# Sigmoid attention into a channel mix on one core: the first block of k in two pieces, narrower products of zeros, and the very last row block in two column halves

## The chip, the cores and the metric

The kernel runs on 1 core of one Trainium2 chip. The metric is the device time of one execution in microseconds (us). The profile is of one execution and counts from the first to the last instruction of the program (the span). Engines are named as the profile names them: PE is TensorE (PEld its weight loads), DVE VectorE, ACT ScalarE, POOL GpSimd, and SP, which here issues nearly all transfers.

## The reference

```python
scores = scale * np.matmul(q, k.transpose(0, 1, 3, 2)) - np.log(S)      # 8 batches, 12 heads, S 448, head 64
attn = 1.0 / (1.0 + np.exp(-scores))
x = np.matmul(attn, v)                                                   # then laid out as 8 x 448 x 768
x_prev = x shifted by one token, zeros first
xk = mu_k * x + (1.0 - mu_k) * x_prev
xr = mu_r * x + (1.0 - mu_r) * x_prev
k = np.maximum(xk @ w_k, 0.0)                                            # 768 -> 1024
v = k * k @ w_v                                                          # 1024 -> 768
r = 1.0 / (1.0 + np.exp(-(xr @ w_r)))                                    # 768 -> 768
return r * v
```

All arrays are float32 (the weights arrive as 64-bit words).

## The kernel before, in words

**Attention.** Two heads lie together in the 128 partitions of one tile, so there are 48 head pairs n; each has its tiles `kn`, `qn` and `vn` of 224 KB. For the first pair (`NATIVE = (0,)`) the scores are multiplied straight in float32; for all others k and q are split into a rounded high part and a low rest (`kh`, `kl`, `qh`, `ql`; type fp32r) and three products are added. `scores(n, c, u, at)` (L349) makes the scores of 128 keys (c = 0, 1, 2) against all 448 queries in the PSUM tile `sc[u]`; `sigmoid` (L373) is one ACT instruction over both heads' 896 columns; `score_tails` and `last_keys` do the last 64 keys of two pairs; `weigh` (L383), `weigh_tails` (L407) and `weigh_last` (L393) multiply with v into `av`; `gather` mixes neighbouring tokens on DVE and stores `xk` and `xr`. Beside it DVE converts the 64-bit weights.

**Channel mix.** Three stages, R (x w_r), K (x w_k), V (x w_v), each as a seven-product scheme for 2 x 2 blocks. A step is (stage, pair of token tiles, product p), with p in the order 0, 1, 5, 4, 6, 2, 3. A step has three row blocks i (four in stage K). `multiply` (L617) makes one row block: in stages R and K 3 x 3, in stage V 4 x 3 matmuls of 128 x 128 weights against T = 448 columns into one PSUM bank (`xb[i]` or `yb[i]`). `yb` gathers the products 0 + 5 + 6 + 3: p = 0 lands in `xb` and ACT copies it to `yb`, the others add to `yb` in place. `evacuate` and `finish` take a finished bank out: in stage V, DVE multiplies it with the stored sigmoid `r` (L648) and SP sends the tile to `out`. The last step is stage V, p = 3; its last row block is `yb[2]`. `yb[3]` is a bank that stage V leaves unused.

**What sets the order.** Nearly every instruction is an `Op` with an engine, an assumed cost, a due time and the tiles that it reads and writes. `Plan.order` plays these through on a list scheduler and the program is emitted in that order; each engine then executes its own list strictly in order and waits on semaphores. So a change of one cost or one added transfer can shift the order of later instructions on any engine. Outside of the plan stand, at the very start, a memset of `warm` (128 x 2, L152), a memset of `mk[1]` (128 x 448, L426), and two matmuls of zeros on 384 columns of `mk[1]` (L428) that keep PE busy until data are there. Then `load(0, ...)` fetches k of the first pair through SP's queue and q through ACT's.

Of the kernel before, what the change touches and what calls it, by code (L numbers as in the profile page):

```python
# [23 lines left out]
class Plan:  # L24
# [9 lines left out]
    def op(self, engine, cost, prio, run, reads, writes, dma=None, gate=False, opens=None):  # L34
        i = len(self.ops)
        deps = set()
        for r in reads:
            if r in self.writer:
                deps.add(self.writer[r])
        for w in writes:  # L40
            if w in self.writer:
                deps.add(self.writer[w])
            deps.update(self.readers.get(w, ()))
        for r in reads:
            self.readers.setdefault(r, []).append(i)
        for w in writes:
            self.writer[w] = i
            self.readers[w] = []
        deps.discard(i)
        self.ops.append(Op(engine, cost, prio, run, deps, dma, gate, opens))  # L50
# [58 lines left out]
def attention_then_channel_mix(  # L109
# [15 lines left out]
    nc = tc.nc  # L125
    P = 128
# [6 lines left out]
    T = S  # L133
# [5 lines left out]
    NJH, NFH = NJ // 2, NF // 2  # L139
# [11 lines left out]
    warm = const.tile([P, 2], F32, name="warm")  # L151
# [13 lines left out]
    WK_PACE, WV_PACE = 1.5, 1.5  # L165
    CAST_DVE = lambda n, a: n % 2 == 1
    NATIVE = (0,)

    def ring(pool, name, bufs, shape, dtype):
        return [pool.tile(shape, dtype, name=f"{name}{i}") for i in range(bufs)]  # L170
# [18 lines left out]
    kn = ring(apool, "kn", RAW, [P, S], F32)  # L189
    vn = ring(apool, "vn", 5, [P, NV, D], F32)  # L190
    gap(apool, "gap1", 64)
    qn = ring(apool, "qn", RAW, [P, S], F32)
# [10 lines left out]
    mk = ring(apool, "mk", 2, [P, S], F32)  # L203
    mr = ring(apool, "mr", 2, [P, S], F32)
    gap(apool, "gap4", 128)
    sc = ring(pscore, "sc", 3, [P, 2, 512], F32)
# [4 lines left out]
    op = plan.op  # L211
    SP, PE, ACT, DVE, POOL = "SP", "PE", "ACT", "DVE", "POOL"
    SWITCH = 92

    def mm(n, cols=S):
        return n * max(cols / 2.4 + 2.5, 200)

    def act(n, sbuf=False, ptr=False):
        return 100 + 0.834 * n + 42 * sbuf + 93 * ptr
# [10 lines left out]
    def dma(dst, src, prio, reads, writes, e="SP"):  # L230
        ns = dst.shape[0] * math.prod(dst.shape[1:]) * 4 / 300
        q_ = nc.scalar if e == ACT else nc.sync
        op(e, 500, prio, lambda: q_.dma_start(dst, src), reads, writes, dma=ns)
# [79 lines left out]
    def load_v(n, at):  # L313
        dma(vn[n % 5], v[n], at, [], [("vn", n % 5)])

    def load(n, at, e="SP", with_v=True):
        dma(kn[n % RAW], k[n], at, [], [("kn", n % RAW)])
        dma(qn[n % RAW], q[n], at, [], [("qn", n % RAW)], e)
        if with_v:
            load_v(n, at)  # L320

    def prepare(n, at):
        if n in NATIVE:
            return
# [8 lines left out]
    half = [slice(h * D, (h + 1) * D) for h in range(2)]  # L333
# [4 lines left out]
    def scores(n, c, u, at):  # L338
        i, m = n % LEAD, n % RAW
        if n in NATIVE:  # L340
            pairs, cost, reads = ((kn[m], qn[m]),), 752, [("kn", m), ("qn", m)]
        else:
            pairs, cost = ((kh[i], qh[i]), (kl[i], qh[i]), (kh[i], ql[i])), 602
            reads = [(a, i) for a in ("kh", "kl", "qh", "ql")]

        def go():
            for e, (kk, qq) in enumerate(pairs):
                for h in range(2):
                    nc.tensor.matmul(sc[u][:, h, :S], kk[half[h], c * P:(c + 1) * P], qq[half[h], :], start=e == 0, stop=e == len(pairs) - 1)  # L349

        pe(cost + 2 * SWITCH * (n % 2 == c == 0), go, reads, [("sc", u, 0), ("sc", u, 1)], at)
# [70 lines left out]
            dma(to[j][:, cols], m, at, [M], [("x", stage, j, b)])  # L422


    zeros = mk[1]
    nc.vector.memset(zeros, 0.0)  # L426
    for _ in range(2):
        nc.tensor.matmul(sc[0][:, 0, :3 * P], zeros[:, :P], zeros[:, :3 * P], start=True, stop=True)  # L428
    load(0, -9, ACT, False)
    op(ACT, 1500, -8.5, lambda: nc.scalar.activation(warm[:, 1:], warm[:, :1], AF.Sigmoid), [], [])  # L430
    load(1, -8, with_v=False)
    load_v(0, -7.8)
# [72 lines left out]
    e = N % RAW  # L505
# [17 lines left out]
    xb, yb = ([[None, (a, i)] for i in range(4)] for a in ("xb", "yb"))  # L523
# [14 lines left out]
    def tokens(tile_):  # L538
        return slice(tile_ * T, (tile_ + 1) * T)
# [63 lines left out]
    def slot_keys(g):  # L603
        return [("slot", g, h) + x for h in range(3) for x in ((), ("lo",))]

    def multiply(stage, s, p, i, at):
        g = POS[p]
        b = (yb if p in (5, 6, 3) else xb)[i]
        rs_ = used[stage, s, p]
        w = CW[stage]  # L610

        def go():
            n = len(rs_)
            for t, (rh, rl, _, _) in enumerate(rs_):
                hi, lo = (slots[g][:, a * n * w + t * w + i * P:a * n * w + t * w + (i + 1) * P] for a in range(2))
                for e, (l, r) in enumerate(((hi, rh), (hi, rl), (lo, rh))):
                    nc.tensor.matmul(b[0], l, r, start=p in (0, 4) and (t, e) == (0, 0), stop=(t, e) == (n - 1, 2), skip_group_check=True)  # L617

        op(PE, mm(3 * len(rs_), T), at, go, [k for r in rs_ for k in r[2:]] + slot_keys(g), [b[1]])


    def finish(stage, s, half, par, i, src, R, c, at):
        in_sbuf = c is not None
        if not in_sbuf:
            u = ncc[0] % len(cc)
            ncc[0] += 1
            c, C = cc[u]
        else:
            C = R[0]
        rows = KT[R_] if stage != K_ else NFH  # L630
        m, tile_ = half * rows + i, PAIRS[s][par]
        cols = tokens(tile_)
        if stage == R_:
            op(ACT, act(T, in_sbuf), at, lambda: nc.scalar.activation(c, src(), AF.Sigmoid), R, [C])
            dma(r_d[m][:, cols], c, at, [C], [("r", m, tile_)])
        elif stage == K_:
            if in_sbuf and half == 0:
                op(DVE, dve(T), at, lambda: nc.vector.scalar_tensor_tensor(c, src(), 0.0, src(), ALU.max, ALU.mult), R, [C])
            else:
                op(ACT, act(T, in_sbuf), at, lambda: nc.scalar.activation(c, src(), AF.Relu), R, [C])  # L640
                op(ACT, act(T, True), at, lambda: nc.scalar.activation(c, c, AF.Square), [C], [C])
            dma(k2_d[m][:, cols], c, at, [C], [("x", V_, m, tile_)])
        else:
            v_ = nrt[0] % len(rt_)
            nrt[0] += 1
            r, G = rt_[v_]
            dma(r, r_d[m][:, cols], at - 1.5, [("r", m, tile_)], [G])
            op(DVE, dve(T), at, lambda: nc.vector.tensor_mul(c, src(), r), R + [G], [C])  # L648
            dma(out[m * P:(m + 1) * P, cols], c, at, [C], [])

    def evacuate(stage, s, p, i, at):
        (_, X), (_, Y), (u, U), (f, F) = (z[i] for z in (xb, yb, u2, p4))
        x, y = (lambda: xb[i][0]), (lambda: yb[i][0])
        if p == 0:
            op(ACT, act(T), at, lambda: nc.scalar.copy(y(), x()), [X], [Y])  # L655
        elif p == 1:
            finish(stage, s, 0, 0, i, x, [X], None, at)
        elif p == 5:
            op(ACT, act(T), at, lambda: nc.scalar.copy(u, y()), [Y], [U])  # L659
        elif p == 4:  # L660
            op(ACT, act(T), at, lambda: nc.scalar.copy(f, x()), [X], [F])
        elif p == 6:
            op(DVE, dve(T), at, lambda: nc.vector.tensor_add(f, y(), f), [Y, F], [F])
            finish(stage, s, 1, 1, i, lambda: f, [F], f, at)
        elif p == 2:
            op(DVE, dve(T), at, lambda: nc.vector.tensor_add(u, x(), u), [X, U], [U])
            finish(stage, s, 0, 1, i, lambda: u, [U], u, at)
        elif p == 3:
            finish(stage, s, 1, 0, i, y, [Y], None, at)

    PREP, EVAC = -1.2, 0.3
    steps = [(stage, s, p) for stage in (R_, K_, V_) for s in range(len(PAIRS)) for p in ORDER]
    first = {stage: next(i for i, x in enumerate(steps) if x[0] == stage) for stage in (R_, K_, V_)}
    last = {(stage, p): max(i for i, x in enumerate(steps) if x[0] == stage and x[2] == p) for stage in (R_, K_, V_) for p in range(7)}
    for stage, w, out7, pace in ((K_, w_k, wk_o, WK_PACE), (V_, w_v, wv_o, WV_PACE)):
        at = OFF + first[stage - 1]
# [3 lines left out]
    for step, (stage, s, p) in enumerate(steps):  # L680
        at = OFF + step
        if (stage, s, p) not in used:
            right(stage, s, p, at + PREP)
        rows = NFH if stage == K_ else NJH
        if step == 3:
            reopen(psa, "pb4", "left", xb[3:] + yb[3:], AV)
        for i in range(rows):
            multiply(stage, s, p, i, at + i / rows)
            evacuate(stage, s, p, i, at + i / rows + EVAC)
        if stage < V_ and last[stage, p] == step:  # L690
            load_weight(stage + 1, p, OFF + max(step + 1.5, first[stage + 1] - 8 + POS[p]))
    ctx.enter_context(tc.manual_schedule())
# [41 lines left out]
```

## Time and profile before

| | |
|---|---|
| median of 3 runs | 807.07 us (806.75, 807.07, 808.11) |
| the profiled execution's own time | 807.04 us |
| its span | 805.0 us |
| PE busy | 800.0 us (99% of the span), 5146 matmuls |
| DVE busy | 620.2 us (77%) |
| ACT busy | 496.8 us (62%) |
| mean granted TensorE clock | 0.999 |
| DMA | 179.76 MB, mean 223 GB/s |

The profile's timeline merges instructions of one kind that follow each other: "x42" after a row means that 42 of them lie between the start and the start plus the duration given. A bracket at a row's end gives the time that the engine was idle before it, and what ended that. "DMA to landing" counts from the issue to the last landing. Bare names such as `pf` or `kn` are tiles without their buffer number.

### The profile page before, as it was taken

How to read it: one execution, taken by the hardware profiler on the slowest of the kernel's cores; microseconds unless marked ns; L12 is line 12 of the kernel's file. 1: busy time of each engine (PE TensorE's matmuls, PEld its weight loads, DVE VectorE, ACT ScalarE, POOL GpSimd, SP SyncE). 2: the span in 40 equal slices, each digit the busy share in tenths (PEclk: the TensorE clock that was granted, in tenths of full speed). 3: DMA queues.
4: the chain of work that ended last, by engine and by line, in shares of the span. 5: the costliest groups of instructions: out<-in, count | busy, mean ns of one | idle time of the engine just before them, and what ended most of it. 6: DMA issues, size and time to landing. Idle time of an engine off the chain costs nothing.

```text
span 805.0 us, 14663 instructions
## 1 busy us (share of the span) xinstructions
PE 800.0 (99%) x5146; PEld 652.7 (81%) x5146; DVE 620.2 (77%) x1161; ACT 496.8 (62%) x857; POOL 8.8 (1%) x29
## 2 busy tenths in 40 slices
PE   9999999999999999999999999999999999999998
PEld 4555555555557999999999999999999999999997
DVE  5888988899898998899988738356597594875944
ACT  6887878877786655556785655657774434344341
POOL 0000000000000000000000000000000000000000
PEclk9999999999999999999999999999999999999999
DMA  8878788798997776768787733434585546655415
GB/s 287 303 235 290 244 257 290 242 315 285 312 320 251 284 234 265 252 216 304 251 292 239 238 118 131 144 109 152 188 265 180 162 158 215 196 193 149 150 46 170
DMA packets 104761, 179.76 MB, mean 223 GB/s; under 512 B 11888, under 2 KB 93296, under 8 KB 104688
## 3 DMA queue, kind: packets, MB, share of 16 engines
q1 hardware_dynamic: 104544, 178.61, 67.3%
q8 instruction: 40, 0.66, 0.3%
q14 instruction: 33, 0.27, 0.1%
q10 hardware_dynamic: 144, 0.23, 0.1%
HBM read 109.06 MB, written 69.73 MB: 222 GB/s over the span
## 4 chain that ended last, share of the span: by engine, by line
PE 99%; DVE 0%; issue 0%
PE pb L617 69%; PE av L383 13%; PE sc L349 10%; PE av L407 2%; PE sc L358 2%; PE av L349 2%; PE av L393 1%; PE sc L428 0%; DVE pt L648 0%; DVE mk L426 0%; DVE warm L152 0%
## 5 line engine op out<-in xcount | busy, mean ns | idle before, releaser
L617 PE MATMUL pb<-rr,slot 128*128 128x448 f32 x2076 | 436.9, 362 | 0.0
L617 PEld LDWEIGHTS pb<-rr,slot 128*128 128x128 f32 x2076 | 389.1, 187 | 26.7 <-issue 0.7
L617 PE MATMUL pb<-qh,slot 128*128 128x448 f32 x464 | 152.6, 363 | 0.0
L383 PE MATMUL av<-pf,vn 64*64 64x448 f32 x1104 | 118.3, 544 | 0.0
L373 ACT ACTIVATE pf<-sc 128x896 f32<-128x896 f32 x120 | 103.9, 961 | 3.2 <-PE sc L349 3.2
L617 PEld LDWEIGHTS pb<-qh,slot 128*128 128x128 f32 x464 | 87.1, 188 | 5.7
L383 PEld LDWEIGHTS av<-pf,vn 64*64 64x64 f32 x1104 | 38.7, 132 | 60.6 <-issue 36.4
L617 PE MATMUL pb<-ql,slot 128*128 128x448 f32 x232 | 83.5, 360 | 0.0
L556 ACT CAST rr<-ys 128x448 fp32r<-128x448 f32 x66 | 36.4, 568 | 47.0 <-PE pb L617 45.1
L557 DVE TENSOR_TENSOR rr<-ys,rr 128x448 fp32r<-128x448 f32 x66 | 39.0, 619 | 12.0 <-ACT rr L556 11.9
L617 PEld LDWEIGHTS pb<-ql,slot 128*128 128x128 f32 x232 | 43.4, 187 | 3.0
L349 PE MATMUL sc<-qh,kh 64*128 64x448 f32 x236 | 45.4, 381 | 0.0
L557 DVE TENSOR_TENSOR rr<-pf,rr 128x448 fp32r<-128x448 f32 x38 | 23.2, 622 | 28.3 <-ACT rr L556 28.3
L417 ACT COPY xx<-av 128x448 f32<-128x448 f32 x48 | 23.3, 539 | 32.3 <-PE av L383 25.3
L349 PE MATMUL sc<-ql,kh 64*128 64x448 f32 x236 | 43.0, 361 | 0.0
L349 PE MATMUL sc<-qh,kl 64*128 64x448 f32 x236 | 42.7, 359 | 0.0
L418 DVE TENSOR_TENSOR dx<-xx 128x448 f32<-128x448 f32 x48 | 29.9, 623 | 14.8 <-ACT xx L417 14.8
L659 ACT COPY pf<-pb 128x448 f32<-128x448 f32 x40 | 21.3, 532 | 32.3 <-PE pb L617 30.2
L655 ACT COPY pb<-pb 128x448 f32<-128x448 f32 x40 | 20.7, 518 | 33.0 <-PE pb L617 33.0
L556 ACT CAST rr<-vn 128x448 fp32r<-128x448 f32 x50 | 27.9, 564 | 18.9 <-PE pb L617 17.6
L349 PEld LDWEIGHTS sc<-qh,kh 64*128 64x128 f32 x236 | 22.1, 184 | 18.2 <-issue 15.5
L557 DVE TENSOR_TENSOR rr<-vn,rr 128x448 fp32r<-128x448 f32 x50 | 29.6, 621 | 6.8 <-ACT rr L556 6.7
(113 smaller groups left out, 1034.1 us busy)
## 6 DMA issues: line engine op xcount, KB each, us to landing
kn<-in_k SPq DMA_DIRECT2D x48, 224.0 KB, 3.9
vn<-in_v SPq DMA_DIRECT2D x48, 224.0 KB, 4.6
xr_d<-mr SPq DMA_DIRECT2D x48, 224.0 KB, 4.7
xk_d<-mk SPq DMA_DIRECT2D x48, 224.0 KB, 4.6
pf<-r_d SPq DMA_DIRECT2D x48, 224.0 KB, 3.3
qn<-in_q SPq DMA_DIRECT2D x47, 224.0 KB, 4.3
k_d<-pf SPq DMA_DIRECT2D x34, 224.0 KB, 2.0
r_d<-pf SPq DMA_DIRECT2D x28, 224.0 KB, 2.4
```

What stands on the lines that cost most here:

```text
L349: nc.tensor.matmul(sc[u][:, h, :S], kk[half[h], c * P:(c + 1) * P], qq[half[h], :], start=e == 0, stop=e == len(pairs) - 1)
L358: nc.tensor.matmul(sc[u][half[m % 2], h, :S], kn[m % RAW][half[h], KW:], qn[m % RAW][half[h], :], start=True, stop=True)
L373: op(ACT, 815, at, lambda: nc.scalar.activation(f, sc[u][:, :, :S], AF.Sigmoid, bias=NEG_LOG_S, scale=SCALE), R, K, opens=opens)
L383: nc.tensor.matmul(av[m % 2][half[h], :S], vn[m % 5][half[r], h * NC + c, :], pf[(m * NC + c) % PFB][half[r], h, :], start=(turn, c) == (0 ...
L407: nc.tensor.matmul(av[r][half[h], :S], vn[(n + h) % 5][half[r], 2 * NC, :], pt[n // 2 % PTB][half[r], h, :], start=False, stop=stop, skip_ ...
L417: op(ACT, act(S), at - 1, lambda: nc.scalar.copy(x[:, 1:], av[n % 2][:, :S]), [AV[n % 2]], [X])
L418: op(DVE, dve(S), at, lambda: nc.vector.tensor_sub(d, x[:, 1:], x[:, :S]), [X], [G])
L556: op(ACT, act(T, True), at, lambda: nc.scalar.copy(hi, y), [Y], [H], gate=True)
L557: op(DVE, dve(T), at, lambda: nc.vector.tensor_sub(lo, y, hi), [Y, H], [L])
L617: nc.tensor.matmul(b[0], l, r, start=p in (0, 4) and (t, e) == (0, 0), stop=(t, e) == (n - 1, 2), skip_group_check=True)
L655: op(ACT, act(T), at, lambda: nc.scalar.copy(y(), x()), [X], [Y])
L659: op(ACT, act(T), at, lambda: nc.scalar.copy(u, y()), [Y], [U])
```

## The change

Three edits:

- **Start.** The matmuls of zeros read one element of `warm` in broadcast, as weights and as moving data, on 320 columns instead of 384. The memset of `mk[1]` is gone. The first k is fetched in two pieces, 128 columns (64 KB) and 320 columns (160 KB); the scores of c = 0 need the first piece alone, those of c = 1 and 2 also the second (key `("kn", 0, 1)`).
- **End.** The last row block of the last step is multiplied in two halves of 224 columns, the first in `yb[2]`, the second in `yb[3]`, each with its own DVE multiplication and its own transfer to `out`. For this ACT copies the right half of the partial sum from `yb[2]` to `yb[3]` two steps before.
- The stored sigmoid of that row block is fetched in two halves as well.

```diff
+    ZEROS = 320
...
+        if n == 0 and c > 0:
+            reads.append(("kn", 0, 1))
...
-    zeros = mk[1]
-    nc.vector.memset(zeros, 0.0)
     for _ in range(2):
-        nc.tensor.matmul(sc[0][:, 0, :3 * P], zeros[:, :P], zeros[:, :3 * P], start=True, stop=True)
-    load(0, -9, ACT, False)
+        nc.tensor.matmul(sc[0][:, 0, :ZEROS], warm[:, :1].to_broadcast([P, P]), warm[:, :1].to_broadcast([P, ZEROS]), start=True, stop=True)
+    dma(qn[0], q[0], -9, [], [("qn", 0)], ACT)
+    dma(kn[0][:, :P], k[0][:, :P], -9, [], [("kn", 0)])
+    dma(kn[0][:, P:], k[0][:, P:], -9, [], [("kn", 0, 1)])
...
+    def multiply(stage, s, p, i, at, cols=slice(0, T), b=None):
         g = POS[p]
-        b = (yb if p in (5, 6, 3) else xb)[i]
+        b = b or (yb if p in (5, 6, 3) else xb)[i]
+        c = cols.stop - cols.start
...
+                    nc.tensor.matmul(b[0][:, :c], l, r[:, cols], start=p in (0, 4) and (t, e) == (0, 0), stop=(t, e) == (n - 1, 2), skip_group_check=True)
...
+    def finish(stage, s, half, par, i, src, R, c, at, part=slice(0, T)):
...
+        cols = slice(tile_ * T + part.start, tile_ * T + part.stop)
+        c = c[:, :part.stop - part.start]
...
+            r = r[:, :part.stop - part.start]
...
         for i in range(rows):
+            if step == len(steps) - 1 and i == rows - 1:
+                for b, cols in ((yb[i], slice(0, T // 2)), (yb[NFH - 1], slice(T // 2, T))):
+                    multiply(stage, s, p, i, at + i / rows, cols, b)
+                    finish(stage, s, 1, 0, i, lambda b=b: b[0][:, :T // 2], [b[1]], None, at + i / rows + EVAC, cols)
+                continue
             multiply(stage, s, p, i, at + i / rows)
             evacuate(stage, s, p, i, at + i / rows + EVAC)
+            if step == len(steps) - 3 and i == rows - 1:
+                a, b = yb[i], yb[NFH - 1]
+                op(ACT, act(T // 2), at + i / rows + EVAC, lambda a=a, b=b: nc.scalar.copy(b[0][:, :T // 2], a[0][:, T // 2:]), [a[1]], [b[1]])
```

The order moves on ACT, DVE and SP in many places, because the plan's times shift by one transfer; on PE it stands as it was but for the first and the last rows. Three places matter for the prediction.

ACT at the start, before (`pf0` to `pf2` are the sigmoids of the first pair, `pt0` those of the last keys of two pairs, `pf3` to `pf5` those of the second pair; `kh0<-kn2` rounds k of the third):

```order
L373 ACTIVATE pf2_169<-av0_189 128x896
L373 ACTIVATE pt0_176<-sc0_186 128x896
L373 ACTIVATE pf3_170<-sc1_187 128x896
L373 ACTIVATE pf4_171<-sc2_188 128x896
L373 ACTIVATE pf5_172<-sc0_186 128x896
L225 CAST kh0_162<-kn2_145 128x384
L225 CAST qh0_157<-qn2_155 128x448
```

The same place after:

```order
L377 ACTIVATE pf2_169<-av0_189 128x896
L377 ACTIVATE pt0_176<-sc0_186 128x896
L226 CAST kh0_162<-kn2_145 128x384
L377 ACTIVATE pf3_170<-sc1_187 128x896
L377 ACTIVATE pf4_171<-sc2_188 128x896
L377 ACTIVATE pf5_172<-sc0_186 128x896
L226 CAST qh0_157<-qn2_155 128x448
```

The cast of the third pair's k has moved ahead of the three sigmoids of the second pair.

SP's queue at the start, before:

```order
L233 DMA kn0_143<-in_k 128x448
L233 DMA kn1_144<-in_k 128x448
L233 DMA qn1_154<-in_q 128x448
L233 DMA vn0_147<-in_v 128x448
L233 DMA vn1_148<-in_v 128x448
```

The whole first k is one issue, with k and q of the second pair behind it. The same queue after:

```order
L234 DMA kn0_143<-in_k 128x128
L234 DMA kn0_143<-in_k 128x320
L234 DMA kn1_144<-in_k 128x448
L234 DMA qn1_154<-in_q 128x448
L234 DMA vn0_147<-in_v 128x448
L234 DMA vn1_148<-in_v 128x448
```

One more issue stands ahead of everything else in that queue.

PE at its end, before (`pb5` is `yb[2]`; `rr`, `qh` and `ql` hold the moving data):

```order
L617 MATMUL pb5_2818<-rr4_128,slot6_122 128x448 x3
L617 MATMUL pb5_2818<-rr5_129,slot6_122 128x448 x3
L617 MATMUL pb5_2818<-qh0_157,slot6_122 128x448
L617 MATMUL pb5_2818<-ql0_159,slot6_122 128x448
L617 MATMUL pb5_2818<-qh0_157,slot6_122 128x448
L617 MATMUL pb5_2818<-qh1_158,slot6_122 128x448
L617 MATMUL pb5_2818<-ql1_160,slot6_122 128x448
L617 MATMUL pb5_2818<-qh1_158,slot6_122 128x448
```

These are twelve matmuls, each with a load of its weights. After, the same twelve stand twice, at 224 columns (`pb41` is `yb[3]`; six rows of the sixteen, where the first half ends and the second begins):

```order
L623 MATMUL pb5_2814<-qh1_158,slot6_122 128x224
L623 MATMUL pb5_2814<-ql1_160,slot6_122 128x224
L623 MATMUL pb5_2814<-qh1_158,slot6_122 128x224
L623 MATMUL pb41_2852<-rr4_128,slot6_122 128x224 x3
L623 MATMUL pb41_2852<-rr5_129,slot6_122 128x224 x3
L623 MATMUL pb41_2852<-qh0_157,slot6_122 128x224
```

The weights of the row block are loaded twice, 24 loads instead of 12.

More of the change, by code (lines that the diff above doesn't have):

```diff
@@ L604, in slot_keys @@
         return [("slot", g, h) + x for h in range(3) for x in ((), ("lo",))]
-    def multiply(stage, s, p, i, at):
+    def multiply(stage, s, p, i, at, cols=slice(0, T), b=None):
         g = POS[p]
-        b = (yb if p in (5, 6, 3) else xb)[i]
+        b = b or (yb if p in (5, 6, 3) else xb)[i]
+        c = cols.stop - cols.start
         rs_ = used[stage, s, p]
@@ L616, in go @@
                 for e, (l, r) in enumerate(((hi, rh), (hi, rl), (lo, rh))):
-                    nc.tensor.matmul(b[0], l, r, start=p in (0, 4) and (t, e) == (0, 0), stop=(t, e) == (n - 1, 2), skip_group_check=True)
-        op(PE, mm(3 * len(rs_), T), at, go, [k for r in rs_ for k in r[2:]] + slot_keys(g), [b[1]])
-    def finish(stage, s, half, par, i, src, R, c, at):
+                    nc.tensor.matmul(b[0][:, :c], l, r[:, cols], start=p in (0, 4) and (t, e) == (0, 0), stop=(t, e) == (n - 1, 2), skip_group_check=True)
+        op(PE, mm(3 * len(rs_), c), at, go, [k for r in rs_ for k in r[2:]] + slot_keys(g), [b[1]])
+    def finish(stage, s, half, par, i, src, R, c, at, part=slice(0, T)):
         in_sbuf = c is not None
@@ L631, in finish @@
         m, tile_ = half * rows + i, PAIRS[s][par]
-        cols = tokens(tile_)
+        cols = slice(tile_ * T + part.start, tile_ * T + part.stop)
+        c = c[:, :part.stop - part.start]
         if stage == R_:
```

## The prediction, written before the changed kernel was run

> **What bounds the kernel now.** I read the page first, for the busy shares and the chain that ended last.
>
> ```profile
> span 805.0 us, 14663 instructions
> PE 800.0 (99%) x5146; PEld 652.7 (81%) x5146; DVE 620.2 (77%) x1161; ACT 496.8 (62%) x857; POOL 8.8 (1%) x29
> PE 99%; DVE 0%; issue 0%
> ```
>
> The chain is PE from end to end. A busy PE need not be a PE at its pace, so I read next the view of waits for PE alone, which has one row, and the timeline of the channel mix, which has long merged pieces.
>
> ```profile
> PE sc L428 <- DVE mk L426: 1.4, 1, 1.4
> ```
> ```profile
> 786.69 8.39 PEld L617 LDWEIGHTS pb<-rr,slot 128*128 128x128 f32 x42
> 786.89 8.56 PE L617 MATMUL pb<-rr,slot 128*128 128x448 f32 x42
> ```
>
> PE waits for another engine only before its first product of zeros (a load's idle time, as in rows below, lies under the matmul ahead of it). In the channel mix 42 loads take 8.39 us, so one matmul of 448 columns passes every (8.39 − 0.19) / 41 = 0.20 us without a gap. Between the first score and the last matmul PE therefore works at its pace; time can be won or lost at the two ends, or by a new stall.
>
> **The start.** The timeline's first microseconds:
>
> ```profile
> 0.73 0.41 ACTq L233 DMA_DIRECT2D qn<-in_q  x1
> 0.74 0.86 SPq L233 DMA_DIRECT2D kn<-in_k  x2
> 0.81 0.06 DVE L152 MEMSET warm<- 128x2 f32 x1 [0.81 <-PEq L704]
> 0.93 0.43 DVE L426 MEMSET mk<- 128x448 f32 x1
> ...
> 1.42 2.93 PE L428 MATMUL sc<-mk 128*128 128x384 f32 x4 [1.42 <-DVE mk L426]
> ...
> 2.22 0.34 PEld L428 LDWEIGHTS sc<-mk 128*128 128x128 f32 x1 [0.30 <-issue]
> ...
> 2.86 0.34 PEld L428 LDWEIGHTS sc<-mk 128*128 128x128 f32 x1 [0.30 <-issue]
> ...
> 4.27 0.51 PEld L349 LDWEIGHTS sc<-qn,kn 64*128 64x128 f32 x4 [1.08 <-DMA qn<-in_q]
> ...
> 4.73 0.36 DVE L225 CAST kh<-kn 128x384 fp32r<-128x384 f32 x1 [3.37 <-DMA kn<-in_k]
> ...
> 5.12 0.56 DVE L330 TENSOR_TENSOR kl<-kn,kh 128x384 fp32r<-128x384 f32 x1
> ...
> 6.02 0.63 DVE L330 TENSOR_TENSOR ql<-qn,qh 128x448 fp32r<-128x448 f32 x1
> 6.05 0.19 PEld L349 LDWEIGHTS av<-qn,kn 64*128 64x128 f32 x2 [0.18 <-issue]
> 6.43 0.19 PEld L349 LDWEIGHTS av<-qn,kn 64*128 64x128 f32 x2 [0.18 <-issue]
> ```
>
> and PE's loads alone from 4.6 on, which keeps the first scores' pairs apart:
>
> ```profile
> 4.44 0.34 PEld L349 LDWEIGHTS sc<-qn,kn 64*128 64x128 f32 x2
> 5.18 0.30 PEld L349 LDWEIGHTS sc<-qn,kn 64*128 64x128 f32 x2 [0.40 <-issue]
> 5.67 0.19 PEld L349 LDWEIGHTS sc<-qn,kn 64*128 64x128 f32 x2 [0.18 <-issue]
> ```
>
> The first score starts at 4.27, when q has landed; k is not named as the last. The products of zeros fill the time until then: their passes are 0.64 us apart (2.22 to 2.86), the last ends near 2.22 + 3 x 0.64 = 4.14. The loads of the first scores are 0.38 us apart at the end (6.05 to 6.43), but here 0.74 (4.44 to 5.18) and then 0.49 (to 5.67): PE runs at half its clock until about 5.41 (the 0.49 are 0.23 at the slow rate and 0.26 at the fast one), 3.99 us after its first work.
>
> *Zeros.* The memset of 0.43 us goes and PE may start after the small one, at 0.81 + 0.06 + 0.05 = 0.92 instead of 1.42. A pass has 320 columns instead of 384, 0.53 us; the zeros end at 0.92 + 0.69 + 3 x 0.53 = 3.2. Broadcast operands appear in no row; their pass costs the 0.53 or, bounded by the old one, 0.64, which only fills idle time. Neither memset nor zeros are on the path, which waits for q.
>
> *k in pieces.* q waits beside k for the same DMA engines. Between 4.34 and 5.40 they move 365 GB/s:
>
> ```profile
> 4.34:5.40 1.06, 1.06 (x5) 0.66 (x6) 0.64 (x2) 0.00 (x0) 0.00 (x0) 1.00 1.04 365
> ```
>
> If the second piece (160 KB) came wholly behind q, q would land 0.44 us earlier; if it shares with q as all of k does now, 0. The second piece is issued 0.4 us later than the first, so part of it follows q: I take the middle, 0.2, the first score at 4.07. PE is at half clock there, so 0.2 us of head start is 0.1 us of work: **−0.1** (0 to −0.2). SP's extra issue (0.43) delays those of kn1 and the rest; the cover is the full DMA queue: kn1, issued at 1.17, lets DVE go only at 4.73. Without that cover, DVE's first casts come 0.4 later, and PE needs them only at 8.18.
>
> *The cast that moved on ACT.* This step is not in the diff but in the order. The place in the timeline before:
>
> ```profile
> 8.18 0.19 PEld L349 LDWEIGHTS sc<-qh,kh 64*128 64x128 f32 x2 [0.70 <-ACT pf L373]
> 8.29 0.19 PEld L349 LDWEIGHTS sc<-qh,kl 64*128 64x128 f32 x2
> ...
> 9.16 2.53 ACT L373 ACTIVATE pf<-sc 128x896 f32<-128x896 f32 x3
> ...
> 10.20 0.21 PEld L383 LDWEIGHTS av<-pf,vn 64*64 64x64 f32 x8 [0.31 <-issue]
> ...
> 11.55 0.53 ACT L225 CAST kh<-kn 128x384 fp32r<-128x384 f32 x1
> ...
> 11.95 0.60 ACT L225 CAST qh<-qn 128x448 fp32r<-128x448 f32 x1
> ```
>
> ACT runs without a gap from pt0 to pf5. The products with v at 10.20 need pf0 and pf3; pf3 is the first of the three from 9.16, spaced (2.53 − 0.92) / 2 = 0.80, done at 10.08. That leaves 0.1 us. The cast, 0.40 us to the next start (11.55 to 11.95), now goes ahead of pf3: pf3 is done at 10.48 and the products wait about 0.3 us. pf4 and pf5 come 0.4 later too but are wanted 0.8 apart behind that stall, so they add nothing. **+0.3** (0, if PE has slack there that I do not see, to +0.4). Nothing gives it back, since PE has no other wait to shorten.
>
> *The other moved instructions* of DVE, ACT and SP: nothing. Their cover is that PE waits for none of them anywhere; where it is gone, one stall is one DVE operation, 0.6.
>
> **The end.** The last 7 us:
>
> ```profile
> 798.89 1.36 PE L617 MATMUL pb<-rr,slot 128*128 128x448 f32 x6
> ...
> 801.09 0.37 PE L617 MATMUL pb<-qh,slot 128*128 128x448 f32 x1
> 801.49 0.62 DVE L648 TENSOR_TENSOR pt<-pb,pf 128x448 f32<-128x448 f32 x1 [1.78 <-PE pb L617]
> ```
> ```profile
> 802.90:803.00 0.10, 0.00 (x0) 0.00 (x0) 0.00 (x0) 0.00 (x0) 0.00 (x0) 1.00 0.27 108
> 803.00:803.75 0.75, 0.00 (x0) 0.00 (x0) 0.00 (x0) 0.00 (x0) 0.00 (x0) 1.00 0.76 292
> 803.75:804.10 0.35, 0.00 (x0) 0.00 (x0) 0.00 (x0) 0.00 (x0) 0.00 (x0) 1.00 0.00 0
> ```
>
> The twelve matmuls of the last row block start at 798.89, the last at 801.09; DVE starts 0.40 behind that, ends at 802.11, and the transfer moves its bytes from 803.00 to 803.75.
>
> *Matmuls.* Twice twelve of 224 columns. Their streaming takes half of 0.19, but each needs a load of 128 x 128 weights. No row has so narrow a matmul. From below: after an idle stretch the second load starts 0.11 us after the first (8.18 to 8.29), so loads cannot follow faster. From above: 0.20, if the pace belongs to the pair and not to the columns. I take 0.12: nearest is the load, 0.11, and the 0.20 holds 0.013 over the 0.1875 that a float32 pass of 448 columns takes (0.375 for two passes, 6.05 to 6.43). The last one starts at 798.89 + 23 x 0.12 = 801.65, and DVE 0.40 − 0.09 = 0.31 behind, at 801.96: +0.47.
>
> *DVE.* 384 columns take 0.56 and 448 take 0.63, 0.07 for 64, so 224 columns save 0.23. *Transfer.* Half the bytes in as many rows: between 0 and half of 0.75 are saved, I take 0.25. The sum of the end is 0.47 − 0.23 − 0.25 = **0.0**; with the bounds from 0.19 − 0.23 − 0.37 = −0.4 (0.11 a matmul) to 2.31 − 0.23 − 0.25 = +1.8 (0.20).
>
> *Beside it.* The first half's multiplication and transfer lie under the second half's matmuls. The added copy on ACT follows its last cast:
>
> ```profile
> 787.09 0.57 ACT L556 CAST qh<-pf 128x448 fp32r<-128x448 f32 x1
> ```
>
> It has 11 us until 798.89. The second half of `r` follows the multiplication of row block 0 (its buffer) and is wanted at 801.96. Both cost 0; each would cost its lateness.
>
> **Sum.** 807.04 (the profiled execution, 805.0 of span and 2.04 around it, 0.03 under the median of 807.07) − 0.1 + 0.3 + 0.0 = **807.2 us**.
>
> **Rivals.**
>
> *The clock comes later (slower).* Before, PE was busy from 1.42 to 5.41 with at most 0.3 us of gap when it got its full clock. After, it idles from 3.2 to 4.07, 0.85 us. If that gap starts the count afresh, full clock comes 3.99 us after 4.07, at 8.06 instead of 5.41: 2.65 us at half rate, +1.3, 808.5. It decides if the gap is long enough to spoil the count, which no row shows. The Trainium skill, "TensorE: Matmul & The Clock Gate", section "Part 1: The HAM clock gate (the "warmup" mystery)", says that the full clock comes after a busy window of about 3.4 us and that these windows run freely, not from the kernel's start; an estimate by it is up to a whole window at half rate, +1.7, against nothing by my sum, and a spread of that size between runs. The trace agrees as far as 3.99 us lies near it.
>
> *Narrow matmuls keep 0.20 us.* Then the end costs +1.8 and the time is 809.0. For it: 0.20 is the only pace of fp32r in the channel mix. Against: the 0.11 between loads.
>
> *The start wins more (faster).* q lands 0.44 earlier, the stall is hidden, 0.11 a matmul: −0.2 + 0 − 0.4, 806.4. For a gain over 0.2% the clock would also have to come before the first score: half of 5.41 − 4.07, another −0.7, 805.7 and still within.
>
> *The reordered DVE and SP lists stall PE* in several of the 24 steps of attention, at 0.6 each, 3 of them +1.8, 809.0. Against it: no wait there before.
>
> **Chances.** Forecast 0.50 (806.8 to 807.8); clock 0.25; narrow matmuls 0.08; stalls 0.05; more won 0.12. A change of 0.2%, 1.6 us, is about what a measurement of this kernel tells from none. Slower by more: the last two slow rivals (0.13) and a part of the clock's (0.07, where it meets its upper price), 0.20; faster by more 0.03; the same 0.77. The range, 806.2 to 808.9, leaves out the two slow rivals of 0.13 and little of the gain.
>
> **What the changed profile would show.** PE's zeros at 0.92 and an idle piece before the first score near 4.07; the spacing of the first scores falling from 0.74 to 0.38 at 5.4 (forecast) or 8 (clock); a wait of 0.3 on ACT's pf before the products with v near 10.3; starts 0.12 apart in the last row block, and its DVE pieces of 0.39. A span that grows in the middle, with waits of PE on DVE, would make the sum wrong.

## The result and the profile after

Ten runs of the changed kernel have a median of 811.74 us (809.12 to 814.45), ten of the kernel before beside them 807.68 us (806.68 to 808.11). The ratio is 1.0053, with a 95% interval of 1.0044 to 1.0062: the change costs about 4 us, where the forecast was 807.2 with a range up to 808.9. The profiled execution took 812.54 us, with a span of 810.4. Only this one of the ten was traced: it and two others (spans of 807.3 us) had a mean granted clock of 1.000, the other seven one of 0.997 or 0.998 (spans of 809.2 to 812.4).

The page of the changed kernel, span, busy times and the chain that ended last:

```profile
span 810.4 us, 14696 instructions
PE 801.0 (99%) x5158; PEld 654.5 (81%) x5158; DVE 620.3 (77%) x1161; ACT 498.3 (61%) x858; POOL 14.0 (2%) x29
PE 96%; issue 2%; POOL 1%; DMA 1%; SPq 0%; DVE 0%; POOLq 0%
```

PE's work grew by 1.0 us, the span by 5.4. POOL, with the same 29 instructions, went from 8.8 us to 14.0, and it now stands in the chain. The first row of PE's waits (us in total, times, longest; the other two, 1.3 us together, lie ahead of the first score):

```profile
PE av L387 <- POOL vn L405: 5.0, 2, 2.9
```

L405 (L401 before) is `end_turn`, which the diff does not touch. Once in each of 23 turns (a turn is two head pairs; the last of the 24 has none) it copies one column of `vn` in place on POOL, between the two halves of the products with v; the second half (L387) reads that tile and so waits for it. The instructions of that line, minimum, median and maximum in ns, first after, then before:

```profile
L405 POOL COPY vn<-vn x23: 184/371/3446, 13.8 to 240.1; 128x1 f32<-128x1 f32 x23
```
```profile
L401 POOL COPY vn<-vn x23: 253/371/434, 13.5 to 234.6; 128x1 f32<-128x1 f32 x23
```

The median is unchanged. Two of the 23 copies took 2.72 and 3.45 us. Here is the first, in the timeline after:

```profile
22.42 0.58 ACT L226 CAST kh<-kn 128x384 fp32r<-128x384 f32 x1
22.50 0.67 DVE L425 SCALAR_TENSOR_TENSOR mk<-dx,muk,xx 128x448 f32<-128x448 f32 x1
...
23.09 0.55 DVE L331 TENSOR_TENSOR kl<-kn,kh 128x384 fp32r<-128x384 f32 x1
...
23.53 0.93 PE L362 MATMUL sc<-qn,kn 64*64 64x448 f32 x8
...
23.56 0.62 DVE L331 TENSOR_TENSOR ql<-qn,qh 128x448 fp32r<-128x448 f32 x1
23.81 2.72 POOL L405 COPY vn<-vn 128x1 f32<-128x1 f32 x1 [9.83 <-PE av L387]
...
25.94 0.55 DVE L248 SCALAR_TENSOR_TENSOR wbits<-wraw,wbits 128x384 uint32<-128x384 uint32 x1
...
26.59 0.61 PE L387 MATMUL av<-pf,vn 64*64 64x448 f32 x4 [2.12 <-POOL vn L405]
...
29.18 0.97 ACT L421 COPY xx<-av 128x448 f32<-128x448 f32 x2 [3.71 <-PE av L387]
...
29.75 0.63 DVE L422 TENSOR_TENSOR dx<-xx 128x448 f32<-128x448 f32 x1 [3.26 <-ACT xx L421]
```

and the same turn before:

```profile
22.16 0.59 ACT L225 CAST kh<-kn 128x384 fp32r<-128x384 f32 x1
...
22.78 0.56 DVE L330 TENSOR_TENSOR kl<-kn,kh 128x384 fp32r<-128x384 f32 x1 [0.45 <-ACT kh L225]
...
23.25 0.62 DVE L330 TENSOR_TENSOR ql<-qn,qh 128x448 fp32r<-128x448 f32 x1
...
23.26 0.93 PE L358 MATMUL sc<-qn,kn 64*64 64x448 f32 x8
...
23.53 0.39 POOL L401 COPY vn<-vn 128x1 f32<-128x1 f32 x1 [9.74 <-PE av L383]
23.79 0.39 DVE L225 CAST qh<-qn 128x448 fp32r<-128x448 f32 x1
...
24.01 2.45 PE L383 MATMUL av<-pf,vn 64*64 64x448 f32 x24
```

The reader is to see three things. Before, DVE was idle for 0.45 us ahead of kl, since ACT was still casting kh; after, other DVE work fills that time, the cast is done at 23.00 and DVE goes from mk to kl without a gap. Before, the copy started within ql and ended 0.05 us behind it (23.25 + 0.62 = 23.87; 23.53 + 0.39 = 23.92). After, it also started within ql but ended only at 26.53, 0.04 us behind the last DVE instruction of a row without a gap (25.94 + 0.55 = 26.49). In all 23 copies before, and in the 21 short ones after, DVE had had a gap in the 1.5 us ahead of the copy; in the two long ones it had had none for 6.4 and 6.1 us. Before, the second half of the products started 0.75 us behind the tails of the scores (23.26 to 24.01); here 3.06 us passed (23.53 to 26.59). That is 2.3 us lost, and 3.1 in the second place. Without them 812.54 − 5.4 = 807.1 remain, close to the forecast's 807.2. From the first of the 23 copies to the last 226.32 us pass instead of 221.02: nearly all of the loss lies there.

The last two rows of the stalled turn tell what ended DVE's row. Its next instruction, dx, waits for ACT's copy xx, and this for PE's products (L387), which wait for POOL. So the copy came through only when DVE had nothing left to do without PE's result; in the second place DVE stops in front of the same instruction, for 3.26 us as well.

The theory for the experiments (A): **DVE working without a gap holds POOL's copy off, and PE waits for the copy.** Rivals: the start or the halved row block costs the time (B); the shifted orders make casts or transfers late (C); something else made the two copies long (D).

### The profile page after: what moved, and what is told of

Same layout as the page of the kernel before. It is cut to its first block, busy times and chain, and to the rows that moved or that the text cites. A ratio compares the mean times of both kernels' runs of the same rounds, so it can differ in the third digit from the quotient of the medians.

```text
span 810.4 us, 14696 instructions
## 1 busy us (share of the span) xinstructions
PE 801.0 (99%) x5158; PEld 654.5 (81%) x5158; DVE 620.3 (77%) x1161; ACT 498.3 (61%) x858; POOL 14.0 (2%) x29
## 4 chain that ended last, share of the span: by engine, by line
PE 96%; issue 2%; POOL 1%; DMA 1%; SPq 0%; DVE 0%; POOLq 0%
PE pb L623 68%; PE av L387 13%; PE sc L353 9%; PE av L411 2%; PE sc L362 2%; PE av L353 2%; POOL vn L405 1%; DMA vn<-in_v 1%; PE av L397 1%; SPq L234 0%; DVE pf L656 0%; POOLq L405 0%
## 5 line engine op out<-in xcount | busy, mean ns | idle before, releaser
L623 PE MATMUL pb<-rr,slot 128*128 128x448 f32 (+1 forms) x2082 | 437.1, 361 | 0.0
L623 PE MATMUL pb<-qh,slot 128*128 128x448 f32 (+1 forms) x468 | 152.9, 361 | 0.0
L387 PE MATMUL av<-pf,vn 64*64 64x448 f32 x1104 | 119.1, 544 | 5.0 <-POOL vn L405 5.0
L387 PEld LDWEIGHTS av<-pf,vn 64*64 64x64 f32 x1104 | 39.7, 132 | 65.3 <-issue 35.5
L623 PE MATMUL pb<-ql,slot 128*128 128x448 f32 (+1 forms) x234 | 83.9, 359 | 0.0
```

The source lines that it names most:

```text
L387: nc.tensor.matmul(av[m % 2][half[h], :S], vn[m % 5][half[r], h * NC + c, :], pf[(m * NC + c) % PFB][half[r], h, :], start=(turn, c) == (0 ...
L623: nc.tensor.matmul(b[0][:, :c], l, r[:, cols], start=p in (0, 4) and (t, e) == (0, 0), stop=(t, e) == (n - 1, 2), skip_group_check=True)
```

## Experiments

**Which part costs the time.** The first k in two pieces alone (the key for c > 0 and the two transfers):

> The kernel before with the first k in two pieces and nothing else; DVE, ACT and SP get the shifted orders of the changed kernel. Theory A (the shifted DVE order leaves POOL's one-column copy behind DVE instructions without a gap, and PE waits for that copy): about 811.9, that is 3 to 6 us above the kernel before, with one to three copies of 2 to 4 us on POOL. Theory B (the start or the halved last row block costs the time): within 0.5 of before. Theory C (the shifted orders make transfers or casts late): also 3 to 6 us above before, but then PE's waits name kl, ql, kh or a load, and the copies last 0.4 us.

811.42 us (809.25 to 812.55), ratio 1.0037 (1.0023 to 1.0051). In its profiled execution, the copies and PE's wait for them:

```profile
L404 POOL COPY vn<-vn x23: 185/369/3099, 14.3 to 240.2; 128x1 f32<-128x1 f32 x23
```
```profile
PE av L386 <- POOL vn L404: 4.7, 2, 2.6
```

One more transfer on SP suffices. That it reaches a turn at 24 us through the order of later instructions is tested by the run after next. The halves alone:

> The kernel before with the last row block in two halves and nothing else; the orders of the score stage are those of before. Theories A and C: 0.1 to 0.3 us below before (the stretch of the last row block was 6.11 us before and 5.95 after). Theory B, in its form that the halves cost the time: 3 to 4 us above before.

807.29 us, ratio 0.9996 (0.9988 to 1.0005): no difference that can be measured, and no loss. Then everything, with the planner seeing one transfer (the key for the second piece goes too, so all scores of the first pair wait for both pieces):

```diff
-    dma(kn[0][:, :P], k[0][:, :P], -9, [], [("kn", 0)])
-    dma(kn[0][:, P:], k[0][:, P:], -9, [], [("kn", 0, 1)])
+    def first_k():
+        nc.sync.dma_start(kn[0][:, :P], k[0][:, :P])
+        nc.sync.dma_start(kn[0][:, P:], k[0][:, P:])
+    op(SP, 500, -9, first_k, [], [("kn", 0)], dma=kn[0].shape[0] * kn[0].shape[1] * 4 / 300)
```

> All three edits, but both pieces of the first k are handed to the planner as one transfer, so that DVE, ACT, POOL and SP keep the order of before. Theory A: no POOL copy over 0.5 us, PE's two stalls of 2.3 and 3.1 us gone, 807.2 to 807.7, 0.0 to 0.4 below before. Theory B (zeros, pieces or halves cost the time by themselves): 811 to 812. Theory C: as A, 807.2 to 807.7.

807.33 us, ratio 0.9998 (0.9989 to 1.0007), with the longest copy at 0.43 us. The edits themselves cost nothing together, and B falls for the whole change. A and C both stand: the order is the cause.

**Is it the copy, or are casts and transfers late?** The changed kernel with the copy taken off POOL:

```diff
-        op(POOL, 200, at, lambda: nc.gpsimd.tensor_copy(u, u), [("vn", m % 5)], [("vn", m % 5)])
+        op(POOL, 200, at, lambda: nc.scalar.copy(u, u), [("vn", m % 5)], [("vn", m % 5)])
```

> The changed kernel with the one-column copy of every turn on ACT instead of POOL; all other orders as in the changed kernel. Theory A: PE no longer waits for POOL, DVE's runs without a gap stay, 806.8 to 807.9. Theory B: 811 to 812. Theory C: 811 to 812, the waits then named at kl, ql, kh or a load.

806.16 us (805.59 to 807.04), ratio 0.9985 (0.9976 to 0.9993). With DVE's and SP's order just as in the changed kernel, all 4 us are gone and about 1 more. C falls as the cause: with the same orders nothing else costs microseconds (the cast that moved on ACT costs 0.3, as shown below). The miss of the expectation is the extra microsecond. Who waited for the copy, in us and times, before and here:

```profile
  PEld av L383: 13.5, 23
```
```profile
  PEld av L387: 8.6, 23
```

PE's first load behind it waits (13.5 − 8.6) / 23 = 0.21 us less in each turn, of which little is PE's own loss, since matmuls still run under it: the median turn takes 10.00 us instead of 10.05. The same move in the kernel before, and with the orders of before kept:

> The kernel before with the one-column copy on ACT instead of POOL and nothing else. In the changed kernel the same move took the copy from 0.37 to 0.19 us in each of 23 turns; if PE waits for it in each turn by that much less, the 21 turns without a long copy are worth up to 3.9 us, but the changed kernel gained only some 1 us beside the two stalls. Expected 0.5 to 1.3 below before, 806.1 to 806.9.

> All three edits with the orders of before kept, and the copy on ACT: the sum of the two moves, 806.0 to 806.7, no better than the changed kernel with the copy on ACT (806.2) by more than 0.3, since with the copy off POOL the order of DVE no longer matters to it.

806.45 us, ratio 0.9991 (0.9982 to 1.0000), and 806.68, 0.9993 (0.9984 to 1.0002). So the medians with the copy on ACT lie 0.5 to 1.3 us below that of the kernel before, whatever the order, though two of the three intervals reach 1. The changed kernel with it is the only version whose whole interval lies below the kernel before; the three of them can't be told apart.

**Can the long copies be made at will?** The kernel before has the short copies; if the gap is what lets POOL in, closing it must make them long. The first try:

```diff
+                if a == "k" and e == ACT:
+                    nc.vector.tensor_sub(lo[i], src, src)
                 nc.vector.tensor_sub(lo[i], src, hi[i])
```

> The kernel before, with one more DVE instruction (a subtraction of 384 columns whose result is overwritten at once, about 0.48 us) ahead of each kl whose kh ACT casts, that is at the place of DVE's idle gap of about 0.55 us ahead of kl; nothing else is changed. Theory A (POOL's copy is held until DVE has a gap): in most of the 23 turns the copy lasts 2 to 4 us and PE waits for it: 20 to 80 us above the kernel before. Rival D (the two long copies came from something else than the missing gap): within 0.5 of before, copies of 0.4 us.

808.95 us, ratio 1.0020 (1.0011 to 1.0029), the longest copy 0.62 us: far from A's 20 us, and outside of rival D's 0.5 us too. But the trace shows that the gap was not closed. kl waits for the added instruction, which writes the same buffer, so that in 20 turns 0.10 us of idleness stayed (0.66 us from start to start instead of 0.47, the 0.19 that the next expectation speaks of), and in the other three more. The run tells only that a gap of 0.10 us close ahead of the copy is enough for POOL. One of the turns:

```profile
52.11 0.56 DVE L333 TENSOR_TENSOR kl<-kn 128x384 fp32r<-128x384 f32 x1
52.77 0.56 DVE L334 TENSOR_TENSOR kl<-kn,kh 128x384 fp32r<-128x384 f32 x1
```

The 1.7 us that this kernel lost in the median are a milder form of the same wait: in its profiled execution 13 copies lasted 0.45 to 0.62 us, and from the first copy to the last 222.4 us pass instead of 221.0. The second try writes to another buffer and is longer:

```diff
+                if a == "k" and e == ACT and n > 2:
+                    x = kn[n % RAW]
+                    nc.vector.scalar_tensor_tensor(ql[i], x, mur[:, :1], x, ALU.mult, ALU.add)
                 nc.vector.tensor_sub(lo[i], src, hi[i])
```

> The kernel before with a longer added DVE instruction (448 columns, about 0.60 us, from the second pair of heads on), written to the buffer of ql instead of kl, so that no wait for it stands ahead of kl: the gap of about 0.55 us ahead of kl is closed in most turns (in gap_filled 0.19 us of it stayed in 16 of 23). Theory A (POOL's copy is held while DVE works without a gap): copies of 2 us and more in at least 5 of the 23 turns, PE waits for each beyond 0.4, 10 to 60 us above the kernel before. Rival D (the missing gap isn't the cause): no copy over 0.7 us and within 1 us of before, the added instructions being 22 x 0.6 us on DVE, for which PE doesn't wait.

861.83 us (861.32 to 866.72), ratio 1.0695 (1.0672 to 1.0718). Rival D falls. The copies and the wait:

```profile
L407 POOL COPY vn<-vn x23: 257/2752/3400, 13.6 to 289.1; 128x1 f32<-128x1 f32 x23
```
```profile
PE av L389 <- POOL vn L407: 37.2, 15, 2.9
```

Fifteen of 23 copies took 2.6 to 3.4 us, and each of the fifteen ended 0.04 to 0.05 us behind a DVE instruction that was followed by a gap. The span grew by 859.5 − 805.0 = 54.5 us. 37.2 of it are these waits. Most of the rest is the clock; two of the stalls by stretches (the columns are the stretch in us, its length, busy time and count of PE, PEld, DVE, ACT and POOL, the granted clock, DMA):

```profile
56.69:60.10 3.41, 1.25 (x16) 0.59 (x20) 2.06 (x6) 0.92 (x1) 2.10 (x1) 1.00 0.68 202
60.10:63.51 3.41, 3.41 (x22) 1.46 (x16) 0.42 (x1) 0.97 (x2) 0.00 (x0) 0.50 0.25 80
159.09:162.50 3.41, 1.39 (x16) 0.31 (x8) 3.41 (x8) 2.19 (x4) 2.62 (x1) 1.00 0.65 218
162.50:165.91 3.41, 2.86 (x28) 1.25 (x30) 0.45 (x1) 0.25 (x1) 0.50 (x1) 1.00 0.65 199
```

PE's wait of 2.16 us in the first stretch is followed by 3.41 us at a granted clock of 0.50. The wait across the third and fourth is 2.57 us, and nothing follows. Nine of the fifteen waits have such a stretch behind them. Over the span the mean clock is 0.982, and 0.018 x 859.5 = 15.5 us is an estimate of what that cost; with the waits that makes 52.7 of the 54.5.

**Any gap, or any instruction of another kind?** The changed kernel with a small DVE instruction behind ql:

```diff
                 nc.vector.tensor_sub(lo[i], src, hi[i])
+                if a == "q" and e == ACT:
+                    nc.vector.tensor_copy(warm[:, 1:], warm[:, :1])
```

> The changed kernel with a copy of one column on DVE (one input, about 0.1 us) behind each ql whose qh ACT casts, right after the place where POOL's copy starts; DVE gets no idle gap by it. If only instructions with two inputs or two streams hold POOL off, and this small one lets it in: no copy over 0.7 us, 806.9 to 807.6. If any DVE instruction without a gap holds it off: two long copies as in the changed kernel, 809 to 812.5.

807.33 us, ratio 1.0001 (0.9992 to 1.0009). The turn that stalled first:

```profile
23.98 0.62 DVE L333 TENSOR_TENSOR ql<-qn,qh 128x448 fp32r<-128x448 f32 x1
24.22 0.42 POOL L411 COPY vn<-vn 128x1 f32<-128x1 f32 x1 [9.82 <-PE av L393]
24.52 0.14 DVE L335 COPY warm<-warm 128x1 f32<-128x1 f32 x1
24.58 0.55 DVE L333 TENSOR_TENSOR kl<-kn,kh 128x384 fp32r<-128x384 f32 x1
```

DVE still goes without a gap, for 6.4 us ahead of the copy and on behind it, and yet the copy ends with ql, at 24.64. The second stalled turn got a gap in this run, so one turn shows it here. The same instruction in the kernel with its gaps closed gives more:

> gap_closed with the one-column copy on DVE behind ql, as in small_op_between. If such an instruction lets POOL in: no copy over 0.7 us, 807 to 808.5. If not: as gap_closed.

809.50 us (808.31 to 809.99), ratio 1.0024 (1.0014 to 1.0034), against 861.8 without it. The longest copy is 0.72 us, though in 13 of the 23 turns DVE had had no gap for 6.4 us or more ahead of the copy. The time is above what I expected. In five turns the copy started close to the end of kl, got in only behind ql and lasted 0.54 to 0.72 us; from these copies to the next 10.2 to 10.4 us pass, where the median turn before takes 10.05.

So it isn't idleness alone that lets POOL in. The DVE instructions around it read two tiles in SBUF or, as the cast and the shifts do, stream 384 or 448 columns from SBUF at about 0.7 ns a column (0.27 us apart for 384, against 0.47 with two inputs). A copy of one column between two of them is enough. The Trainium skill, "Advanced Engine Details and Errata", section "VectorE Performance Modes", says that VectorE's second SBUF port is shared with GPSIMD and that two-port instructions and GPSIMD's block each other; "GPSIMD Engine Reference", section "8. Key points", adds the instructions with two SBUF inputs. The runs agree with both, and give what neither states: a copy of 0.37 us that lasts up to 3.45.

**The zeros alone.**

> The kernel before with the narrower products of zeros on the small tile alone; all orders are kept. Theory A: no long copy; the products of zeros start at 0.92 instead of about 1.4, which nothing waits for, 807.0 to 807.9, no difference that can be measured. Theory B (the narrower products bring the full clock later): 0.4 us more at the first loads, up to 808.3.

808.75 us (807.55 to 809.42), ratio 1.0017 (1.0009 to 1.0026): slower than both theories had it. Its weight loads, and those of the changed kernel:

```profile
4.37 0.51 PEld L349 LDWEIGHTS sc<-qn,kn 64*128 64x128 f32 x4 [1.88 <-DMA qn<-in_q]
...
6.77 0.34 PEld L349 LDWEIGHTS av<-qn,kn 64*128 64x128 f32 x2 [0.41 <-issue]
7.52 0.34 PEld L349 LDWEIGHTS av<-qn,kn 64*128 64x128 f32 x2 [0.41 <-issue]
...
10.20 0.19 PEld L349 LDWEIGHTS sc<-qh,kh 64*128 64x128 f32 x2 [0.75 <-ACT pf L373]
```
```profile
0.92 2.50 PE L430 MATMUL sc<-warm 128*128 128x320 f32 x4 [0.92 <-DVE warm L152]
...
3.80 2.74 PE L353 MATMUL sc<-qn,kn 64*128 64x448 f32 x8 [0.38 <-DMA qn<-in_q]
```
```profile
4.71 0.34 PEld L353 LDWEIGHTS sc<-qn,kn 64*128 64x128 f32 x2 [0.41 <-issue]
5.46 0.34 PEld L353 LDWEIGHTS sc<-qn,kn 64*128 64x128 f32 x2 [0.41 <-issue]
6.00 0.19 PEld L353 LDWEIGHTS av<-qn,kn 64*128 64x128 f32 x2 [0.21 <-issue]
6.38 0.19 PEld L353 LDWEIGHTS av<-qn,kn 64*128 64x128 f32 x2 [0.19 <-issue]
...
8.13 0.19 PEld L353 LDWEIGHTS sc<-qh,kh 64*128 64x128 f32 x2 [0.70 <-ACT pf L377]
```

With the zeros alone, PE is idle from 3.42 to 4.37, because q still lands as late as with k in one piece. The pairs are then still 0.75 us apart at 7.52, the slow rate, where before they were 0.38 apart from 6.05 on; the first product of the split scores comes at 10.20 instead of 8.18. In the profiled execution of the changed kernel q lands at 3.80, the idle piece is 0.38 us, the spacing falls behind 5.46, and that product comes at 8.13. But one execution does not tell what a start does. The run with the orders of before kept starts with the same edits, and there the pairs are still at the slow rate at 7.02:

```profile
6.27 0.34 PEld L350 LDWEIGHTS av<-qn,kn 64*128 64x128 f32 x2 [0.41 <-issue]
7.02 0.34 PEld L350 LDWEIGHTS av<-qn,kn 64*128 64x128 f32 x2 [0.41 <-issue]
```

Its idle piece is 0.45 us and its first split product comes at 9.14. With the start of before, in the run with the halves alone, that product comes at 9.09 instead of 8.18.

What decides can be read from the traces' records of the granted clock (ahead of the first record the views print 1.00). The first record, of the full clock, is at 5.41 us in the kernel before, 5.79 in the changed one, 7.18 with the halves alone, 7.75 with the orders kept and 9.50 with the zeros alone. Count back from it in stretches of 3.41 us, the length of the half-clock stretches above: in all 13 traces PE is busy for at least 3.03 us of the last stretch and for at most 2.97 of any earlier one. With the orders kept the stretch that ends at 4.34 has 2.97; with the zeros alone the one that ends at 6.08 has 2.46.

So the forecast's first rival, a later clock, is real for the zeros alone: an idle piece of 0.95 us is more than the about 0.4 that a stretch can lose. With k in pieces the idle piece is about that 0.4, and how the stretches fall decides.

## Why the prediction was wrong

- **The step that failed** is "The other moved instructions of DVE, ACT and SP: nothing", with "one stall is one DVE operation, 0.6" behind it. Its cover, that PE waits for none of them, was read from a trace with the old order. The wait that came is not for DVE but, through DVE, for POOL, and one stall costs 2.3 to 3.1 us. The rival with reordered lists had the right origin, but the wrong engine and about a quarter of the price of a stall or less, and got 0.05. The orders compared ahead of the prediction are those of ACT, SP and PE; it was DVE's that decided.
- What could have been read before: POOL's copy stands between two halves of PE's work in every turn, and each of its 23 copies ended about 0.04 us behind a DVE instruction. PE's loads waited for that copy 23 times, 13.5 us in all (the row above); the prediction set the idle time of loads aside as lying under a matmul. An engine whose 0.37 us follow another's ends is tied to it; the sum costed POOL's list as if it were free.
- **Zeros:** they start at 0.92, as forecast. That they cost nothing holds in the median of the run with the orders kept, where all three edits together take 807.33 us against 807.43; alone they cost about 1.6 us through the clock.
- **k in pieces, −0.1:** the first score came 0.47 us earlier (4.27 to 3.80), a little more than the upper bound and not the middle. The full clock came later, behind 5.46: of the 0.54 us to the load at 6.00, 0.33 are at the slow rate, so at 5.79 instead of 5.41. At half rate the two leave −0.235 + 0.19 = −0.05, which is what the load at 8.13 instead of 8.18 shows. That this lies so near −0.1 is luck: with the clock at 7.75, as with the orders kept, the same start comes out 1 us late (9.14). The prediction took the 3.99 us from PE's first work to the full clock for a count that starts with that work; in the traces they are 3.1 us (the first try at closing the gap) to 8.6 (the zeros alone). In the run with the pieces alone the first score still starts at 4.27, since the zeros fill PE until then: for an earlier first score the two edits need each other.
- **The cast on ACT, +0.3:** right, and by the mechanism named. It went ahead of pf3, and of the first eight products with v the four that need pf3 start 0.34 us behind the others, which stretches their row from 0.98 to 1.31 us. The rows after, then before:

```profile
10.15 1.31 PE L387 MATMUL av<-pf,vn 64*64 64x448 f32 x8
...
16.65 0.47 PE L353 MATMUL sc<-qh,kh 64*128 64x448 f32 x2
```
```profile
10.20 0.98 PE L383 MATMUL av<-pf,vn 64*64 64x448 f32 x8
...
16.37 0.47 PE L349 MATMUL sc<-qh,kh 64*128 64x448 f32 x2
```

  From the first split product of this turn to the first of the next 16.65 − 8.13 = 8.52 us pass, before 16.37 − 8.18 = 8.19: +0.33. With the halves alone, the orders kept and the zeros alone, where ACT keeps its order of before, it is 8.18 to 8.20.
- **The end, 0.0:** −0.13. The rows answer to those of the last 7 us:

```profile
804.45 0.82 PE L623 MATMUL pb<-rr,slot 128*128 128x224 f32 x6
...
807.01 0.27 PE L623 MATMUL pb<-qh,slot 128*128 128x224 f32 x1
807.32 0.39 DVE L656 TENSOR_TENSOR pf<-pb,pf 128x224 f32<-128x224 f32 x1 [0.89 <-PE pb L623]
807.74 0.33 SPq L234 DMA_DIRECT2D out<-pf  x1
```

  A matmul of 224 columns takes (807.01 − 804.45) / 23 = 0.111 us, the lower bound and not the 0.12; DVE starts 0.31 behind the last and takes 0.39, as forecast. From the first matmul to the end of the span, which is 810.39 and was 804.96, 5.94 us pass instead of 6.07. One figure of the bounds was off: 23 matmuls of 0.11 us put DVE's start at 801.73, 0.24 behind the old one and not 0.19; the lower bound stays at −0.4.

The terms that the prediction did cost thus came to −0.05 + 0.33 − 0.13 = +0.15 us, against its +0.2. The term that it put at nothing cost about 5.3 us in the profiled execution. What stays open: how many stalls the nine other executions had, and how much of their time is the clock; and the exact rule by which POOL gets in. In the kernel with closed gaps two copies were short (0.44 and 0.38 us) though DVE's last gap, of less than 0.1 us, lay 3.2 to 3.3 us back, and two others with a wider gap as far back were long. Whether the one-column copy helps by its single input or by its shortness wasn't separated either.

## What to carry to other kernels

An instruction on POOL that another engine waits for can cost what is left of DVE's run without a gap, not its own time; the run can even end only where DVE itself waits for that engine; look for such waits before costing a new order, and put a small instruction that must come in time on ACT, or a one-column one between DVE's long ones. Where a planner sets the order, one added transfer can move idle time that something depended on: compare the places where an engine was idle, not only those where it was waited for. And filler work ahead of a clock change has to last until real work starts; when it is shortened, what it covered has to come earlier by as much. One execution does not show what such an edit is worth: the same start had its full clock at 5.79 us in one and at 7.75 in another.

## What the runs showed of the hardware that I had not expected

- A POOL copy of one column, 0.37 us as a rule, lasted up to 3.45 us beside DVE instructions without a gap, and ended 0.04 us behind the last of them. A gap of 0.10 us, or one DVE copy of one column, was enough to let it in.
- A stall costs clock by where it falls. In the kernel with closed gaps all changes of the granted clock lie on one grid of 3.41 us. In attention, from the first full clock on, a stretch at 0.50 followed each of the nine stretches of the grid in which PE was busy for 1.37 us or less, and none with 1.39 or more: a wait of 2.16 us inside one stretch brought it, one of 2.57 us across two did not. In the profiled execution of the changed kernel the least is 1.47 us, and its waits of 2.1 and 2.9 us left the mean clock at 1.000. The Trainium skill, "TensorE: Matmul & The Clock Gate", section "Part 1: The HAM clock gate (the "warmup" mystery)", says that the clock follows windows of about 3.4 us that run freely. The length and the grid agree with that; the busy shares that decide, here and at the start, are from these traces.
